# Thresholded attention and leaky-ReLU MoE on one core: fixed issue order, both heads through one clamped fp16 tile, reciprocal sums turned along with the weights

## The chip, the cores and the metric

The kernel runs on one core of one Trainium2 chip. The metric is the device time of one execution in microseconds (us). Each run has a state: slow when it is over 1.5% above the fastest run of the same kernel, else fast.

Engines are named as the profile names them: PE (matmul), PEld (its weight load), DVE (vector), ACT (scalar), POOL (GpSimd), SP (issues most DMAs). A name with a q behind it (SPq) is the engine's queue of DMA issues.

## The reference

Shortened: `scale` is 1 over the root of the head size, and type casts are left out.

```python
def _attn_ref(q, k, v, tau):                     # q, k, v: (8, 8, 576, 64)
    scores = scale * np.matmul(q, k.transpose(0, 1, 3, 2))
    thresh = np.max(scores, axis=-1, keepdims=True) - tau
    scores = np.where(scores >= thresh, scores, -1000000000.0)
    scores = scores - np.max(scores, axis=-1, keepdims=True)
    attn = np.exp(scores)
    attn = attn / (np.sum(attn, axis=-1, keepdims=True) + 1e-09)
    return np.matmul(attn, v)

def _moe_ref(x, w_in, w_out):                    # (4608, 512) x (512, 2048) x (2048, 512)
    h = x @ w_in
    return np.maximum(0.01 * h, h) @ w_out
```

The attention output, heads side by side, is x of the second part.

## The kernel before

The work is cut into 144 steps. A step takes 128 query rows of two heads (or the last 64 rows of four heads): scores on PE, the row maximum on DVE, a thresholded exponential, a DMA transpose of the weights ("turn"), and, LAG = 4 steps later, the weighted sum of v (`pv`) on PE. Units of the MoE part (`h_unit`, `o_unit`) fill PE between the scores. q and k of the next batch are split into a high and a low fp16 part and turned by DMA while a batch runs. A batch has 18 steps; a batch border is where the scores go on to the next batch's q and k.

The two heads of a step go different ways. Head 0 gets an Exp of the fp32 scores on ACT and is masked by a multiply on DVE. Head 1 is scaled into an fp16 tile P, clamped on DVE through its int16 view, and gets its Exp afterwards. POOL then multiplies both by the reciprocal of the row sum.

```python
    def tmax(sc, f):                              # row "maximum", as a minimum of the negated scores
        ...
        nc.vector.tensor_scalar(
            out=halves(ns), in0=sc[:, :, 0:288], scalar1=-C, scalar2=None, op0=AX.mult, op1=AX.min, accum_out=mn)
        nc.vector.tensor_scalar(out=bi, in0=mn, scalar1=tau_f, scalar2=f, op0=AX.add, op1=AX.mult)

    def norm(s):
        ...
        nc.vector.reciprocal(out=rc, in_=sm)
        for h in range(2):
            nc.gpsimd.tensor_scalar(out=W[:, h, :], in0=W[:, h, :], scalar1=rc[:, h : h + 1], ...)
        wt = sb.tile([128, 9, 128], FP16, tag="wt", bufs=LAG, name="wt")
        nc.sync.dma_start(out=wt, in_=W.rearrange("p h k -> p (h k)"), transpose=True)
        ...

    for s in range(NS + LAG + 1):
        ...                                       # credit: how many MoE units this step takes
        if live:
            ...                                   # tiles; those of E and P below are left out too
            scores(s, sc)
            nsa, ba = tmax(sc[0], 1.0)
            nc.scalar.activation(out=E, in_=nsa, func=AF.Exp, bias=ba, scale=-1.0)
            nsb, bb = tmax(sc[1], KD)
            nc.scalar.activation(out=P, in_=nsb, func=AF.Identity, bias=bb, scale=-KD)
        ...                                       # pv(s - LAG), o units, h units
        if 0 <= s - 1 < NS:
            norm(s - 1)
        if live:
            nc.vector.scalar_tensor_tensor(       # mask-multiply of head 0
                out=d["W"][:, 0, :], in0=nsa, scalar=ba, in1=E,
                op0=AX.is_le, op1=AX.mult, accum_out=d["sm"][:, 0:1])
        ...                                       # eviction of pv to xT on ACT; preparation of the next batch
        if live:
            nc.vector.tensor_scalar(out=pi, in0=pi, scalar1=NEG, scalar2=None, op0=AX.max)   # clamp
            nc.scalar.activation(
                out=d["W"][:, 1, :], in_=P, func=AF.Exp, bias=0.0, scale=1.0 / KD, accum_out=d["sm"][:, 1:2])
```

A scheduler orders the instructions of each engine; program order is only its input. At the start all q and k of batch 0 are loaded, split and turned in two halves before the first scores, while POOL issues the loads of v and of both MoE weights.

The names of tiles in the profile: `km`, `qm` are k and q as loaded; `ks`, `qs` their two fp16 parts; `kst`, `qst` these turned, the operands of the scores. `sc` are the scores, `ns` (before) or `sf` (after) the scaled scores, `mn` or `mx` the row minimum or maximum, `bi`, `ba` and `bb` biases made from it, `E` an exponential, `P` the fp16 tile of the clamp. `w` are the weights, `wt` the turned weights, `sm` and `rc` the row sum and its reciprocal, `pv` the weighted sum and `xT` its copy, the input of the MoE part. `win` and `wout` are the MoE weights, `wio` their product, `hp`, `gT`, `op` and `osb` the intermediate and output tiles of the MoE part.

## Time and profile before

| | before |
|---|---|
| time, median of the first 3 runs | 778.84 us (774.13 to 784.93) |
| profiled span | 779.7 us |
| first scores start / last clamp starts | 45.05 / 733.4 us |
| mean granted TensorE clock | 0.914 |

The first part of the page lists the busy time of each engine, its share of the span and its number of instructions. The second part gives forty equal slices; a digit is a share in tenths.

```profile
PE 596.9 (77%) x5520; PEld 345.8 (44%) x5520; DVE 479.0 (61%) x1489; ACT 450.6 (58%) x814; POOL 364.1 (47%) x406
...
PEclk9999988879788598989997899899998999999999
DMA  9999999995895919599478975985479654444511
```

No engine is saturated, and the granted clock dips in the first half. So the time is not the work of one engine. It is what the steps wait for.

Groups of instructions of the kernel before: line, engine, operation, output and inputs with shapes, count, then busy us and mean ns of one, then idle us just before them and who ended it.

```profile
L344 POOL TENSOR_SCALAR w<-w,rc 128x576 f16<-128x576 f16 x288 | 231.6, 816 | 301.6 <-DVE bi L335 175.2
L332 DVE TENSOR_SCALAR_CACHE_REDUCE ns<-sc 128x576 f32<-128x576 f32 x288 | 207.2, 747 | 48.8 <-PE sc L278 44.2
...
L423 DVE SCALAR_TENSOR_TENSOR w<-ns,bi,E 128x576 f16<-128x576 f32 x144 | 162.0, 1125 | 107.9 <-ACT E L411 91.2
...
L432 DVE TENSOR_SCALAR P<-P 128x576 int16<-128x576 int16 x144 | 67.6, 469 | 8.7 <-ACT P L414 8.6
```

DVE spends 162 us on the mask-multiply (L423) and waits another 91 us for E before it. The clamp (L432) has a mean of 469 ns, but its median is 302 and its longest 2460. That is the mark of something that holds it up from outside.

The timeline of the kernel before, an undisturbed step: start, duration, engine, line, operation, and in brackets the idle time before it.

```profile
559.17 1.33 DVE L423 SCALAR_TENSOR_TENSOR w<-ns,bi,E 128x576 f16<-128x576 f32 x1 [0.78 <-ACT E L411]
...
560.43 0.30 DVE L432 TENSOR_SCALAR P<-P 128x576 int16<-128x576 int16 x1
560.65 0.74 DVE L332 TENSOR_SCALAR_CACHE_REDUCE ns<-sc 128x576 f32<-128x576 f32 x1
...
561.33 0.75 DVE L332 TENSOR_SCALAR_CACHE_REDUCE ns<-sc 128x576 f32<-128x576 f32 x1
...
563.05 1.33 DVE L423 SCALAR_TENSOR_TENSOR w<-ns,bi,E 128x576 f16<-128x576 f32 x1 [0.78 <-ACT E L411]
```

The mask-multiply recurs after 3.88 us: two maxima, a wait of 0.78 us for E, the multiply, the clamp, one after the other on DVE. Over the whole run a step takes about 4.8 us, so some 0.9 us per step are lost to other waits.

A count of clamps in a window counts steps. Windows of the kernel before, for the clamp alone: the window and its length, busy us of DVE with the number of clamps (x), then granted clock, DMA share (it can read a little above 1) and GB/s of the core in that window.

```profile
0.00:100.00 100.00, 5.98 (x12) 0.98 1.06 185
100.00:160.00 60.00, 7.47 (x12) 0.81 1.00 164
```

### The profile page before, as it was taken

To read this page: it belongs to the slowest core of one execution; us is meant where nothing else is said; L and a number is where in the kernel's file an instruction comes from. 1 tells how busy PE (TensorE), PEld (TensorE's weight loads), DVE (VectorE), ACT (ScalarE), POOL (GpSimd) and SP (SyncE) were. 2 spreads that over 40 slices of the span, in tenths; PEclk is the share of its full clock that TensorE was granted. 3 is DMA by queue.
4 is the path that set the end of the run, shared out by engine and by line. 5 is a ranking of instruction groups with operands and counts; after the bars stand their busy time and mean duration, and the time that the engine had idled before them with its cause. 6 is when DMAs were issued, how large, how long until landed. Compare 5 with 4: busy or idle time off the path is not lost. (4 is left out here: it accounts for less than half of the span.)

```text
span 779.7 us, 15311 instructions
## 1 busy us (share of the span) xinstructions
PE 596.9 (77%) x5520; PEld 345.8 (44%) x5520; DVE 479.0 (61%) x1489; ACT 450.6 (58%) x814; POOL 364.1 (47%) x406
## 2 busy tenths in 40 slices
PE   0038768688688998778867898679857888888997
PEld 0014334445445454344544455345534545554663
DVE  1058558587384575566656887477755887787501
ACT  2046556675465475575656676576755767676731
POOL 4118557676465443665346633593345333333300
PEclk9999988879788598989997899899998999999999
DMA  9999999995895919599478975985479654444511
GB/s 194 198 189 165 177 183 173 128 182 148 135 172 131 137 30 156 94 180 173 92 119 147 179 117 113 153 144 113 93 120 150 105 103 84 85 90 90 91 41 41
DMA packets 280460, 101.67 MB, mean 130 GB/s; under 512 B 256832, under 2 KB 267072, under 8 KB 280384
## 3 DMA queue, kind: packets, MB, share of 16 engines
q1 hardware_dynamic: 268992, 91.78, 65.8%
q0 software_dynamic: 11392, 8.92, 7.9%
q8 instruction: 43, 0.70, 0.4%
q14 instruction: 33, 0.27, 0.1%
HBM read 36.70 MB, written 9.44 MB: 59 GB/s over the span
## 5 line engine op out<-in xcount | busy, mean ns | idle before, releaser
L344 POOL TENSOR_SCALAR w<-w,rc 128x576 f16<-128x576 f16 x288 | 231.6, 816 | 301.6 <-DVE bi L335 175.2
L278 PE MATMUL sc<-kst,qst 64*128 64x288 f16 x1536 | 175.3, 313 | 103.6 <-DVE ns L332 56.8
L332 DVE TENSOR_SCALAR_CACHE_REDUCE ns<-sc 128x576 f32<-128x576 f32 x288 | 207.2, 747 | 48.8 <-PE sc L278 44.2
L423 DVE SCALAR_TENSOR_TENSOR w<-ns,bi,E 128x576 f16<-128x576 f32 x144 | 162.0, 1125 | 107.9 <-ACT E L411 91.2
L278 PEld LDWEIGHTS <-qst 64*128 64x128 f16 x1536 | 93.5, 101 | 176.0 <-issue 105.5
L170 PE MATMUL hp<-xT,win 128*128 128x256 f16 (+1 forms) x1216 | 157.6, 277 | 11.1 <-ACT gT L188 10.2
L170 PE MATMUL op<-wout,gT 128*128 128x512 f16 x576 | 159.5, 400 | 0.0
L411 ACT ACTIVATE E<-ns,bi 128x576 f16<-128x576 f32 x144 | 110.9, 770 | 69.7 <-DVE bi L335 68.9
L433 ACT ACTIVATE w<-P 128x576 f16<-128x576 f16 x144 | 98.0, 681 | 83.3 <-issue 29.5
L170 PEld LDWEIGHTS <-win 128*128 128x128 f16 x1216 | 115.8, 101 | 56.5 <-issue 21.9
L414 ACT ACTIVATE P<-ns,bi 128x576 f16<-128x576 f32 x144 | 109.6, 761 | 10.3 <-DVE rc L342 7.5
L302 PE MATMUL pv<-wt,v 128*64 128x128 f16 (+1 forms) x1600 | 72.7, 235 | 52.0 <-DMA wt<-w 37.6
L188 ACT ACTIVATE gT<-hp 128x512 f16<-128x512 f32 x144 | 83.2, 581 | 49.8 <-PE hp L170 42.8
L302 PEld LDWEIGHTS <-v 128*64 128x64 f16 x1600 | 54.5, 120 | 88.2 <-issue 69.0
L170 PEld LDWEIGHTS <-gT 128*128 128x128 f16 x576 | 57.8, 101 | 62.2 <-issue 13.1
L432 DVE TENSOR_SCALAR P<-P 128x576 int16<-128x576 int16 x144 | 67.6, 469 | 8.7 <-ACT P L414 8.6
L110 ACT ACTIVATE ks<-km 128x640 f16<-128x640 f32 (+1 forms) x32 | 20.9, 674 | 67.5 <-DMA kst<-ks 55.7
L170 PE MATMUL op<-wio,xT 128*128 128x512 f16 x144 | 58.3, 405 | 2.1 <-DVE osb L207 2.1
L207 DVE COPY osb<-op 128x512 f32<-128x512 f32 x36 | 24.8, 688 | 47.5 <-PE op L170 47.5
L342 DVE RECIPROCAL rc<-sm 128x2 f32<-128x2 f32 x144 | 22.5, 156 | 40.7 <-ACT w L433 39.9
L335 DVE TENSOR_SCALAR bi<-mn 128x1 f32<-128x1 f32 x288 | 39.0, 141 | 0.2
L129 POOL TENSOR_TENSOR ks<-km,ks 128x640 f16<-128x640 f32 (+1 forms) x28 | 38.6, 1395 | 0.7
(31 smaller groups left out, 290.3 us busy)
## 6 DMA issues: line engine op xcount, KB each, us to landing
km<-in_k_dram SPq DMA_DIRECT2D x32, 288.0 KB, 4.7
qm<-in_q_dram SPq DMA_DIRECT2D x32, 288.0 KB, 4.7
out_dram<-osb SPq DMA_DIRECT2D x36, 256.0 KB, 2.7
v<-in_v_dram POOLq DMA_DIRECT2D x16, 160.0 KB, 6.0
wt<-w SPq DMA_TRANSPOSE x144, 3.5
v<-in_v_dram POOLq DMA_DIRECT2D x16, 128.0 KB, 7.3
win<-in_moe_w_in_dram POOLq DMA_DIRECT2D x4, 512.0 KB, 18.5
wout<-in_moe_w_out_dram POOLq DMA_DIRECT2D x4, 512.0 KB, 23.3
```

Of the source, the lines that this page charges most:

```text
L170: nc.tensor.matmul(out=out_, lhsT=lhsT, rhs=rhs, start=start, stop=stop, skip_group_check=True)
L188: nc.scalar.activation(out=G.g[:, ds(u * per, per), :], in_=hp, func=AF.Relu, bias=0.0, scale=0.99)
L278: nc.tensor.matmul(out=sc[h][:, half, 0:288], lhsT=qsts[b, p][r, qi, ds(128 * c, 128)], rhs=ksts[b, p][r, ki, ks_], start=(i == 0), stop=( ...
L302: nc.tensor.matmul(out=pvp[ds(64 * h, 64), p + u, :], lhsT=vt[:, p + u, h, j, :], rhs=wt[:, 4 * h + j, ds(64 * u, n)], start=(j == 0), sto ...
L332: nc.vector.tensor_scalar(out=halves(ns), in0=sc[:, :, 0:288], scalar1=-C, scalar2=None, op0=AX.mult, op1=AX.min, accum_out=mn)
L335: nc.vector.tensor_scalar(out=bi, in0=mn, scalar1=tau_f, scalar2=f, op0=AX.add, op1=AX.mult)
L344: nc.gpsimd.tensor_scalar(out=W[:, h, :], in0=W[:, h, :], scalar1=rc[:, h : h + 1], scalar2=1.0, op0=AX.mult, op1=AX.mult)
L411: nc.scalar.activation(out=E, in_=nsa, func=AF.Exp, bias=ba, scale=-1.0)
L414: nc.scalar.activation(out=P, in_=nsb, func=AF.Identity, bias=bb, scale=-KD)
L423: nc.vector.scalar_tensor_tensor(out=d["W"][:, 0, :], in0=nsa, scalar=ba, in1=E, op0=AX.is_le, op1=AX.mult, accum_out=d["sm"][:, 0:1])
L432: nc.vector.tensor_scalar(out=pi, in0=pi, scalar1=NEG, scalar2=None, op0=AX.max)
L433: nc.scalar.activation(out=d["W"][:, 1, :], in_=P, func=AF.Exp, bias=0.0, scale=1.0 / KD, accum_out=d["sm"][:, 1:2])
```

## The change

Its intent: take POOL out of the weight chain; send both heads the same way, so that one wide clamp serves both and DVE has no mask-multiply; and write the order of each engine's instructions by hand. In its core, with cuts:

```diff
+    ctx.enter_context(tc.manual_schedule())
 ...
+        if 0 < s <= NS:                           # the step before: one clamp and two Exp for both heads
+            anchor[0] = nc.vector.tensor_scalar(out=pi, in0=pi, scalar1=NEG, scalar2=None, op0=AX.max)
 ...
+            for h in range(2):
+                nc.scalar.activation(
+                    out=e["W"][:, ds(576 * h, 576)], in_=e["P"][:, h, :], func=AF.Exp, bias=exp_bias, scale=1.0,
+                    accum_out=sm[:, h : h + 1])
         if live:
-            nsa, ba = tmax(sc[0], 1.0)
-            nc.scalar.activation(out=E, in_=nsa, func=AF.Exp, bias=ba, scale=-1.0)
-            nsb, bb = tmax(sc[1], KD)
-            nc.scalar.activation(out=P, in_=nsb, func=AF.Identity, bias=bb, scale=-KD)
+            sa, ma = smax(s, 0, sc[0])
+            sB, mb = smax(s, 1, sc[1])
 ...
+            nc.vector.tensor_scalar(              # head 0 into P on DVE
+                out=d["P"][:, 0, :], in0=sa, scalar1=ma, scalar2=tau_f, op0=AX.subtract, op1=AX.add)
+            nc.scalar.activation(out=d["P"][:, 1, :], in_=sB, func=AF.Identity, bias=bb, scale=1.0)
 ...
-            nc.gpsimd.tensor_scalar(out=W[:, h, :], in0=W[:, h, :], scalar1=rc[:, h : h + 1], ...)
-        wt = sb.tile([128, 9, 128], FP16, tag="wt", bufs=LAG, name="wt")
+            nc.vector.tensor_scalar(              # reciprocals, spread over a tenth block of W
+                out=e["W"][:, 1152:1280].rearrange("p (h r) -> p h r", h=2),
+                in0=rc.unsqueeze(2).to_broadcast([128, 2, 64]), scalar1=1.0, scalar2=None, op0=AX.mult)
+            turn_w(s - 1)                         # turns 10 blocks
 ...
-                nc.scalar.activation(out=xo, in_=xi, func=AF.Copy, bias=0.0, scale=1.0)
+                nc.vector.tensor_tensor(          # eviction times the turned reciprocals
+                    out=x_, in0=pvp.rearrange("f g (i p) -> f g i p", i=2),
+                    in1=wts[0][:, :, 9, :].rearrange("f g (i p) -> f g i p", i=2), op=AX.mult)
```

Also: output tiles (osb) are copied by ACT instead of DVE; POOL's splitting is tied behind the clamp (`after_anchor`); q and k are loaded and split pair by pair at the start, partly on DVE; the weight loads stand behind POOL's splitting in POOL's queue:

```diff
-    for hb in range(2):
-        load_half(k, kms, "km", 0, hb)
-        load_half(q, qms, "qm", 0, hb)
+    for p in range(NP):
+        load_pair(k, kms, "km", 0, p)
+        load_pair(q, qms, "qm", 0, p)
 ...
             t0 = s0 + 9 * hb                      # when the next batch's loads are issued
 ...
+            t0 = s0 + 1 + 8 * hb                  # when its halves are split and turned
 ...
         at(1 + g // 2, lambda g=g: load_w_in(g))
         at(3 + g // 2, lambda g=g: load_w_out(g))
```

## The prediction

> **What bounds it now.** The busy table (779.7 us span) shows no saturated engine: PE 597, DVE 479, ACT 451, POOL 364 us. There are 144 softmax steps; the first scores start at 45 us, the last end near 729: 4.75 us per step. An undisturbed stretch of the timeline (559 to 567 us) runs at 3.9 us per step, paced by DVE: two 0.68 us maxima, 0.1 of bias, 0.78 waiting for ACT's E, a 1.33 us mask-multiply, the 0.3 us clamp. The other 0.85 us are stalls: in-order queues blocked behind operand preparation and DMA transposes. In the table of waits DVE waits 91 us for E, PE 38 for turned weights and 57 for the maxima, ACT 56 for kst transposes. DMA share is about 1.0 from 50 to 180 us. The granted clock in 2 us windows is 1.00 or 0.50, halved after PE gaps (0.50 at 582 us, after 578 to 582 idle). The Trainium skill, "TensorE: Matmul & The Clock Gate", Part 1, says idleness halves the clock and activity releases it; this trace agrees.
>
> **What changes, per step.**
> - DVE loses the mask-multiply (162 us in all, plus its wait for E) and 25 us of osb copies. It gains P from an fp32 tile (estimate 0.4 us, from the Trainium skill, "VectorE: DVE Perf Modes", the tier table: fp32 SBUF scalar ops run two per cycle), a clamp twice as wide (0.3 to about 0.45), a 128x128 reciprocal broadcast (about 0.25) and, each fourth step, the xT multiply (about 0.75). About 2.9 us busy.
> - ACT trades one fp32 Exp (0.77) for an fp16 Exp with accumulator (0.78), and xT evictions for osb copies: about 3.2 us.
> - POOL loses 232 us of normalisation, so less contention with the clamp (median 302 ns, mean 469, worst 2460).
> - The wt transpose grows from 9 to 10 blocks: about 22 us more DMA in total. All DMA is then about 600 us by the present accounting (74% of 780 plus 22), but late windows move 205 GB/s per unit of share against 176 overall, so about 520 at best: the new second limit.
> - PE work is the same (scores 0.84, pv 0.40, o 1.10, h 0.96 at full clock: 3.3 us per step, about 490 altogether), with fewer gaps, so the clock should rise.
>
> **Critical path.** The weight chain loses POOL (1.46 us plus its queue). DVE's loop falls from 3.9 to about 3.0, and PE (3.3), ACT (3.2) and DMA (3.6) set the pace: 3.9 us per step with residual stalls. Pairwise loads, splitting on DVE, and weight loads queued behind POOL's splitting should bring the first scores from 45 to about 18 us. Tail about 48 as before (same units left after the last scores). Sum: 18 + 144 x 3.9 + 48 = 628 us.
>
> **Predicted: 628 us, 580 to 690.** Faster 0.96, same 0.03, slower 0.01.
>
> **Signs.** Right: first scores before 22 us; POOL busy near 130 us, DVE near 440, ACT near 450; clamp about 0.45 us with few long ones; clock at least 0.95; PE share above 88%; DMA share above 85%. Wrong if pv's waits for wt grow, ACT and DVE lock-step near 4.5 us through clamp and P, or POOL's splitting, now tied to the clamp, makes kst late at batch borders.
>
> **What would make it wrong.** DMA transposes saturating (above 650); fixed order exposing each late semaphore; or a near-dense PE (about 580).

## The result, and the profile after

| | before | after |
|---|---|---|
| time, median (same rounds) | 778.48 us | 667.08 us (664.01 to 670.47) |
| ratio of fast runs, 95% interval | 1 | 0.8564 (0.8491 to 0.8638) |
| mean granted clock | 0.914 | 0.958 |
| first scores / last clamp start | 45.05 / 733.4 us | 16.68 / 618.1 us |

A ratio is the mean time of one kernel's fast runs over that of the kernel before's fast runs of the same rounds, so it is not quite the ratio of the medians.

The page after, its first two parts:

```profile
PE 528.4 (79%) x5584; PEld 317.2 (48%) x5584; DVE 433.9 (65%) x1358; ACT 446.9 (67%) x955; POOL 150.4 (23%) x200
...
PEclk9999979989898989799998989999989998999999
DMA  9999999999999999979996999999998999557301
```

POOL lost 214 us of work and DVE 45, and the clock dips less. The busy share of the DMA is now above 90% in most slices nearly to the end.

Groups after:

```profile
L363 DVE TENSOR_SCALAR_CACHE_REDUCE sf<-sc 128x576 f32<-128x576 f32 x288 | 206.5, 754 | 133.8 <-PE sc L303 122.8
L481 ACT ACTIVATE w<-P 128x576 f16<-128x576 f16 x288 | 193.6, 675 | 29.6 <-DVE P L477 16.9
...
L490 DVE TENSOR_SCALAR P<-sf,mx 128x576 f16<-128x576 f32 x144 | 73.8, 512 | 0.0
...
L477 DVE TENSOR_SCALAR P<-P 128x1152 int16<-128x1152 int16 x144 | 66.0, 459 | 11.0 <-ACT P L492 4.1
...
L496 DVE TENSOR_SCALAR w<-rc 128x128 f16<-128x128 f32 x144 | 32.8, 228 | 5.1
```

The clamp is twice as wide and its mean is no longer than before (459 against 469 ns). The maxima now wait for PE's scores (123 us, before 44), so DVE no longer sets the pace by itself.

The timeline after, a step without a stall:

```profile
400.26 0.91 PE L303 MATMUL sc<-kst,qst 64*128 64x288 f16 x12
...
401.89 0.75 DVE L363 TENSOR_SCALAR_CACHE_REDUCE sf<-sc 128x576 f32<-128x576 f32 x1
...
402.75 0.51 DVE L490 TENSOR_SCALAR P<-sf,mx 128x576 f16<-128x576 f32 x1
...
403.56 0.91 PE L303 MATMUL sc<-kst,qst 64*128 64x288 f16 x12
...
403.68 0.46 DVE L477 TENSOR_SCALAR P<-P 128x1152 int16<-128x1152 int16 x1
...
404.50 0.76 DVE L363 TENSOR_SCALAR_CACHE_REDUCE sf<-sc 128x576 f32<-128x576 f32 x1 [0.36 <-PE sc L303]
```

Scores recur after 3.30 us and PE is dense between them, while DVE waits 0.36 us for them. But the windows, again for the clamp, show that the first steps were slow:

```profile
0.00:100.00 100.00, 4.48 (x9) 0.97 1.09 168
100.00:160.00 60.00, 6.84 (x15) 0.94 0.97 170
```

At 100 us the changed kernel had done 9 steps, the one before 12, although its first scores came 28 us earlier. (Counted by scores instead of clamps, which run a step later in the changed kernel, it is 10 against 13.) From there to the last clamp it did 135 steps in 518 us, 3.84 us each; the kernel before did 132 in 633 us, 4.80 each. The whole gain, and more, is made after 100 us.

The timeline after shows the start:

```profile
16.68 1.62 PE L303 MATMUL sc<-kst,qst 64*128 64x288 f16 x12 [16.68 <-DMA kst<-ks]
...
36.12 19.23 SPq L377 DMA_TRANSPOSE wt<-w  x2
43.32 1.62 PE L303 MATMUL sc<-kst,qst 64*128 64x288 f16 x12 [16.21 <-DMA qst<-qs]
47.87 1.25 ACT L125 ACTIVATE ks<-km 128x640 f16<-128x640 f32 x2 [21.78 <-DMA km<-in_k_dram]
...
66.05 0.75 PE L327 MATMUL pv<-wt,v 128*64 128x128 f16 x10 [8.51 <-DMA wt<-w]
```

PE stands 16 us for a turn of batch 0, ACT 22 us for a load of batch 1 that stands ahead of its Exp in the fixed order, and PE again for turned weights. The issue of two turns took 19 us. A turn of weights lands in 4.4 us at the median, in 20.1 at the worst.

Later there is a stall at every batch border, for instance here:

```profile
489.54 1.44 SPq L144 DMA_TRANSPOSE qst<-qs  x1
...
493.97 1.51 PE L303 MATMUL sc<-kst,qst 64*128 64x288 f16 x12 [2.54 <-DMA qst<-qs]
...
495.51 0.76 DVE L363 TENSOR_SCALAR_CACHE_REDUCE sf<-sc 128x576 f32<-128x576 f32 x1 [4.80 <-PE sc L303]
```

The turn of q that these scores need is issued at 489.54, only 4.4 us before they start. PE idles 2.5 us for it, and DVE then 4.8 us for the scores.

### The profile page after: what moved, and what is told of

Its sections match the earlier page's. It is cut to its first block, busy times and chain, and to the rows that moved or that the text cites. A ratio compares the mean times of both kernels' runs of the same rounds, so it can differ in the third digit from the quotient of the medians.

```text
span 666.1 us, 14773 instructions
## 1 busy us (share of the span) xinstructions
PE 528.4 (79%) x5584; PEld 317.2 (48%) x5584; DVE 433.9 (65%) x1358; ACT 446.9 (67%) x955; POOL 150.4 (23%) x200
## 3 DMA queue, kind: packets, MB, share of 16 engines
q0 software_dynamic: 11392, 8.92, 10.9%
## 4 chain that ended last, share of the span: by engine, by line
PE 51%; DMA 22%; DVE 12%; ACT 9%; SPq 3%; issue 2%; POOL 0%; ACTq 0%
PE op L189 19%; PE hp L189 14%; DMA wt<-w 13%; PE sc L303 10%; DVE sf L363 8%; PE pv L327 5%; DMA qst<-qs 5%; ACT P L492 3%; DMA km<-in_k_dram 3%; ACT w L481 3%; PE wiop L189 2%; DVE P L477 2%; SPq L79 1%; ACT ks L125 1%; PE sc L309 1%
## 5 line engine op out<-in xcount | busy, mean ns | idle before, releaser
L363 DVE TENSOR_SCALAR_CACHE_REDUCE sf<-sc 128x576 f32<-128x576 f32 x288 | 206.5, 754 | 133.8 <-PE sc L303 122.8
L481 ACT ACTIVATE w<-P 128x576 f16<-128x576 f16 x288 | 193.6, 675 | 29.6 <-DVE P L477 16.9
L303 PE MATMUL sc<-kst,qst 64*128 64x288 f16 x1536 | 132.0, 302 | 75.2 <-DMA qst<-qs 45.3
L492 ACT ACTIVATE P<-sf,bb 128x576 f16<-128x576 f32 x144 | 111.4, 773 | 78.0 <-DVE bb L488 72.7
L327 PE MATMUL pv<-wt,v 128*64 128x128 f16 (+1 forms) x1600 | 71.2, 224 | 48.4 <-DMA wt<-w 45.7
L490 DVE TENSOR_SCALAR P<-sf,mx 128x576 f16<-128x576 f32 x144 | 73.8, 512 | 0.0
L477 DVE TENSOR_SCALAR P<-P 128x1152 int16<-128x1152 int16 x144 | 66.0, 459 | 11.0 <-ACT P L492 4.1
L137 POOL TENSOR_TENSOR ks<-km,ks 128x320 f16<-128x320 f32 (+1 forms) x64 | 47.2, 758 | 92.6 <-DVE P L477 61.3
L137 POOL TENSOR_TENSOR qs<-qm,qs 128x576 f16<-128x576 f32 x28 | 35.8, 1278 | 87.0 <-DVE P L477 55.6
L481 ACT ACTIVATION_READ_ACCUMULATOR w<-P 128x1 f32 x288 | 54.8, 190 | 0.0
L496 DVE TENSOR_SCALAR w<-rc 128x128 f16<-128x128 f32 x144 | 32.8, 228 | 5.1
```

Source lines behind the costliest of these rows:

```text
L137: return nc.gpsimd.tensor_tensor(out=dst[:, h], in0=src[:, h], in1=h_[:, h], op=AX.subtract)
L303: nc.tensor.matmul(out=sc[h][:, half, 0:288], lhsT=qsts[b, p][r, qi, ds(128 * c, 128)], rhs=ksts[b, p][r, ki, ks_], start=(i == 0), stop=( ...
L327: nc.tensor.matmul(out=pvp[ds(64 * h, 64), p + u, :], lhsT=vt[:, p + u, h, j, :], rhs=wt[:, 4 * h + j, ds(64 * u, n)], start=(j == 0), sto ...
L363: nc.vector.tensor_scalar(out=halves(sf), in0=sc[:, :, 0:288], scalar1=C, scalar2=None, op0=AX.mult, op1=AX.max, accum_out=mx)
L477: anchor[0] = nc.vector.tensor_scalar(out=pi, in0=pi, scalar1=NEG, scalar2=None, op0=AX.max)
L481: nc.scalar.activation(out=e["W"][:, ds(576 * h, 576)], in_=e["P"][:, h, :], func=AF.Exp, bias=exp_bias, scale=1.0, accum_out=sm[:, h : h ...
```

## The experiments

The questions: why did the start give nothing (39 us over the prediction in all), what holds the steady steps above 3.3 us, and which part of the change made the gain. Every kernel differs from the changed one by the edit shown. Twelve kernels ran, in four groups; kernels of one group share their runs of the kernel before.

| run | edit | median us | ratio to before (95%) |
|---|---|---|---|
| changed kernel | | 667.08 | 0.8564 (0.8491 to 0.8638) |
| x1 | no weight loads (wrong) | 643.65 | 0.8286 (0.8162 to 0.8410) |
| x2 | batch 1 prepared later | 668.62 | 0.8616 (0.8551 to 0.8681) |
| x3 | scheduler's order | 705.09 | 0.9095 (0.9014 to 0.9176) |
| x4 | LAG 6 | 665.05 | 0.8568 (0.8502 to 0.8634) |
| x5 | batches 2 to 7 prepared 3 steps earlier | 646.02 | 0.8238 (0.8190 to 0.8286) |
| x6 | less DMA (wrong) | 647.55 | 0.8288 (0.8259 to 0.8318) |
| x7 | POOL normalises again | 672.66 | 0.8620 (0.8590 to 0.8650) |
| x8 | POOL not tied to the clamp | 674.37 | 0.8631 (0.8607 to 0.8655) |
| x9 | head 0 the old way | 680.24 | 0.8741 (0.8680 to 0.8802) |
| x10 | x5, weights and MoE later | 662.94 | 0.8500 (0.8428 to 0.8571) |
| x11 | x10, batch 1 later | 658.22 | 0.8435 (0.8367 to 0.8503) |
| x12 | x1 and x5 (wrong) | 623.35 | 0.8018 (0.7978 to 0.8058) |

The changed kernel was not run again beside these. A difference to it is one of medians from different groups, and the kernel before's medians range over these groups from 778.1 to 781.9 us: read differences as good to a few us. In the group of x1 to x4 three of the seven runs of the kernel before were slow and left out, and the record calls these four verdicts unclear; the intervals of x1 and x3 still do not touch the changed kernel's, while those of x2 and x4 overlap it.

### x1: no weight loads

```diff
+    nc.gpsimd.memset(w_in16.rearrange("p a b -> p (a b)").bitcast(FP32), 0.0)
+    nc.vector.memset(w_out16.rearrange("p a b -> p (a b)").bitcast(FP32), 0.0)
 ...
-        at(1 + g // 2, lambda g=g: load_w_in(g))
-        at(3 + g // 2, lambda g=g: load_w_out(g))
```

> Wrong on purpose: both MoE weight tiles are set to zero by two memsets at the start and never loaded; all else is as in the changed kernel. Theory A (the 39 us missing at the start go to the weight loads, which fill the DMA while the first steps need it): by 100 us at least 17 steps are done instead of about 10, transposes of the first steps land in about 5 us instead of 15 to 20, time near 635 us. Rival B (the in-order queues block on the next batch's k and q loads and splits, whatever the weights do): time stays above 655 us, ACT still waits about 20 us for km at step 1.

643.65 us, 23 less. The windows of this kernel, for the clamp:

```profile
0.00:100.00 100.00, 7.96 (x16) 1.00 1.01 169
100.00:160.00 60.00, 6.84 (x15) 0.91 1.04 168
```

16 steps are done at 100 us instead of 9, and after that the pace is the same (15 clamps in 60 us in both). So the weight loads cost the start seven steps. The slowest turn of `wt` landed after 10.3 us instead of 20.1; the medians are 4.3 and 4.4. The zeros in the weight tiles did not free the clock: it was 0.964 over the run (0.958 with weights), and 0.91 against 0.94 from 100 to 160 us. It is not all of theory A's claim, which had at least 17 steps and a time near 635 us: ACT still waited 13.0 us for the km of batch 1, so part of what rival B named remains once the weights are gone.

### x2: batch 1 prepared later

```diff
             t0 = s0 + 9 * hb
+            if b == 1:
+                t0 = 10 + 3 * hb
 ...
-            t0 = s0 + 1 + 8 * hb
+            t0 = s0 + (5 if b == 1 and hb == 0 else 1 + 8 * hb)
```

> The k and q loads of batch 1 are issued from step 3 on instead of step 0, and its first half is split from step 5 on instead of step 1; weights as in the changed kernel. Theory B (ACT, and behind it DVE and PE, stand in the fixed order behind the split of a km that has not landed): the 21.8 us wait of ACT for km is gone and time falls by 15 us or more, to 650 or less. Theory A (the DMA is full anyway with weights): the wait moves to the wt transposes and time falls by less than 8 us.

668.62 us: no gain. ACT's wait of 21.8 us is gone (one of 10.5 us for the same km came later, at 70 us), and in its place the issue of three turns took 31.4 us (19.2 for two in the changed kernel), the slowest turn of `wt` landed after 29.9 us, and ACT stood 16.6 us for a bias of DVE, which stood 16.5 us for PE's scores, which stood 17.7 us for a qst. With the weights in the way, reordering what stands behind them moves the wait and does not shorten it. Of the two theories, A is the one that fits this run.

### x3: the scheduler orders again

```diff
-    ctx.enter_context(tc.manual_schedule())
 ...
-        if anchor[0] is not None:
+        if False:
```

> The changed kernel with the scheduler ordering the instructions again (no fixed order, no ties of GpSimd work to the clamp). If the fixed order is a large part of the gain: slower by 5% or more, 700 us or above, with PE clock below 0.94 and steps in the steady part above 4.2 us. If the lighter arithmetic is nearly all of the gain: 655 to 685 us.

705.09 us, 38 more than the changed kernel and some 74 less than the one before. With the scheduler the first clamp came after 50 us, as in the kernel before; DVE waited 93.5 us for ACT's P in front of the clamp (4.1 in the fixed order); and PE's clock was 0.937. From 160 to 580 us it did 99 steps, 4.24 us each, where the changed kernel did 108. At 100 us it had done 12 steps, three more than the changed kernel, so what the fixed order gains is gained after the start. About a third of the 111 us needs the fixed order (with the ties to the clamp, which this run also drops), and two thirds come without it.

### x4: more lag

```diff
-    LAG = 4
+    LAG = 6
-    NWT = 2
+    NWT = 3
```

(with one or two buffers fewer for sf, osb, P, xT and mx, to make room)

> The weighted sum runs 6 steps behind the scores instead of 4 (third buffer of turned weights; sf, osb, P, xT and mx each with one or two buffers fewer to make room). If pv's 46 us of waits for wt are a matter of latency, they fall below 15 us and time by 15 us or more, to 650 or less. If the DMA's throughput sets the pace from 100 to 580 us, time changes by less than 1% and the waits move elsewhere (qst, kst, wt buffers).

665.05 us: within noise. The wait that it was aimed at did shrink: the waits of PE's `pv` for wt fell from 45.7 us to 7.0. The time did not, and the waits of the scores for qst grew from 45.3 to 65.1 us. Taking the wait for turned weights away thus did not make the steps faster. This outcome is the one expected of a DMA whose throughput sets the pace; x5 speaks against that reading. Whether the smaller buffers took back part of what the lag gave was not run apart.

### x5: the next batch prepared three steps earlier

```diff
-            t0 = s0 + 9 * hb
+            t0 = s0 + 9 * hb - (3 if b > 1 else 0)
 ...
-            t0 = s0 + 1 + 8 * hb
+            t0 = s0 + 1 + 8 * hb - (3 if b > 1 else 0)
```

> For batches 2 to 7 the k and q loads, splits and turns all sit three steps earlier; batch 1, at the start, is untouched. If the waits of the scores for qst at the batch borders (4 to 6 us in each of seven places on the chain of waits) are lateness in the fixed order, they vanish for six of them and time falls by 15 to 25 us, to 642 to 652. If the DMA's throughput is the limit from 100 to 580 us, the time moves by less than 1% and the waits go to wt.

646.02 us, 21 less, and correct: this version beats both kernels. (One of its four runs, at 649.38 us, is slow and left out of the ratio.) Who waited for whom: total us, times, longest us. First the changed kernel:

```profile
PE sc L303 <- DMA qst<-qs: 45.3, 10, 16.2
```

then this one:

```profile
PE sc L303 <- DMA qst<-qs: 21.8, 4, 13.9
```

Eight of the ten waits in the changed kernel stand at the borders into batches 1 to 7 (one of 2.2 to 5.4 us at each, and another of 1.1 at one of them). In this run only the border into batch 1, which the edit leaves alone, still has any (4.5 and 0.4 us); the other two are at the start. Windows of the changed kernel, for the clamp, and then of this one:

```profile
160.00:580.00 420.00, 49.26 (x108) 0.95 1.02 173
```

```profile
160.00:580.00 420.00, 52.92 (x116) 0.98 1.05 179
```

Eight more steps fit into the same 420 us, at 3.62 us each instead of 3.89. The clock is higher and the DMA moves more per second. (The profiled run, 639.39 us, is the fastest of the four and 1% below their median, so this window flatters the edit a little.) A DMA share of 1.0 was thus no proof of a full DMA: the same queues carried 3% more when the turns were asked for earlier. The waits at the borders were lateness.

### x6: less DMA

```diff
-        nc.sync.dma_start(out=d["wt"], in_=d["W"], transpose=True)
+        nc.sync.dma_start(out=d["wt"][:, 0:9, :], in_=d["W"][:, 0:1152], transpose=True)
 ...
-                    in1=wts[0][:, :, 9, :] ...
+                    in1=wts[0][:, :, 8, :] ...
 ...
+        if b > 1:
+            vts[b] = vbufs[b % 2]                 # v of batches 2 to 7 is not loaded
```

> Wrong on purpose: the tenth block is computed but not turned (9 blocks again), the eviction multiplies by the ninth, and v of batches 2 to 7 is not loaded. That takes about 4.7 MB of transposes and 3.5 MB of loads off the DMA, some 8% of its bytes, and no instruction off PE, DVE or ACT. If the DMA's throughput sets the pace of the steady part, steps get 5 to 8% shorter there: time 625 to 642. If PE and the interlocks between the engines set it, time stays within 1.5% of the changed kernel.

647.55 us, 20 less: between the two expectations, nearer the first. Bytes on the DMA fell by 8%, time by 3%; from 160 to 580 us a step took 3.72 us instead of 3.89, 4% less, where 5 to 8% were expected of a DMA that sets the pace. A turn of weights also lands a little sooner (4.2 us at the median instead of 4.4), so bandwidth and lateness are not separated by this run alone. The DMA matters in the steady part, but its bytes do not set the pace one for one.

### x7: POOL normalises again

```diff
-            nc.vector.tensor_scalar(out=e["W"][:, 1152:1280]..., in0=rc.unsqueeze(2).to_broadcast([128, 2, 64]), ...)
+            for h in range(2):
+                w_ = e["W"][:, ds(576 * h, 576)]
+                nc.gpsimd.tensor_scalar(out=w_, in0=w_, scalar1=rc[:, h : h + 1], scalar2=1.0, op0=AX.mult, op1=AX.mult)
 ...
-                nc.vector.tensor_tensor(out=x_, in0=pvp..., in1=wts[0][:, :, 9, :]..., op=AX.mult)
+                nc.vector.tensor_copy(out=x_, in_=pvp...)
```

> One part of the change undone: GpSimd normalises the weights again (2 x 144 instructions of about 0.75 us), 9 blocks are turned, the eviction is a plain DVE copy. If taking GpSimd out of the chain[...] is what the tenth block is worth: slower by 2% or more (680 us and above), clamps longer than 0.6 us on average. If the transposes' bytes weigh more: same or faster (650 to 668).

672.66 us, a ratio 0.7% above the changed kernel's with overlapping intervals: not told apart from no difference, and in neither of the two expected ranges. The group lines of this kernel:

```profile
L493 POOL TENSOR_SCALAR w<-w,rc 128x576 f16<-128x576 f16 x288 | 238.7, 841 | 225.3 <-DVE rc L490 224.5
...
L472 DVE TENSOR_SCALAR P<-P 128x1152 int16<-128x1152 int16 x144 | 107.8, 749 | 28.7 <-ACT P L487 26.6
```

The contention is real: the same clamp takes 749 ns on average instead of 459 with POOL's multiplies back, its longest 2924. P from the fp32 tile went from 512 to 598 ns, while the maxima, which read the scores from PE's accumulator memory (PSUM), stayed at 751 (754). The Trainium skill, "SBUF — State Buffer", section "SBUF: two separate sides", says that the port pair shared by GpSimd and Vector is an exclusive lock held for the whole instruction; this agrees. It costs hardly any time here. The likely reasons are that a DVE that waits for PE has room for 0.3 us more per step, and that the tenth block's own bytes are saved; they were not tested apart.

### x8: POOL not tied to the clamp

```diff
-        if anchor[0] is not None:
+        if False:
```

(in `after_anchor` only; the order stays fixed)

> The ties of GpSimd's splitting to the clamp are left out; nothing else. If they keep the wide clamp from waiting behind GpSimd: clamps with a mean above 0.55 us and some above 1.5 us, time slower by 1 to 3%. If they only delay the splits: same or a little faster.

674.37 us, a ratio 0.8% above, again with overlapping intervals. The mechanism was partly wrong: the clamp grew only from 459 to 498 ns, and the longest was 1025, not above 1500. The other DVE instructions in its neighbourhood took more of it (P from 512 to 593 ns, the spread of reciprocals from 228 to 323). A small cost at most; not settled.

### x9: head 0 the old way

```diff
-            nc.vector.tensor_scalar(
-                out=d["P"][:, 0, :], in0=sa, scalar1=ma, scalar2=tau_f, op0=AX.subtract, op1=AX.add)
+            nc.scalar.activation(out=d["E"], in_=sa, func=AF.Exp, bias=ba, scale=-1.0)   # sa: negated scores
 ...
+            nc.vector.scalar_tensor_tensor(       # one step later, so it need not wait for E
+                out=e["W"][:, 0:576], in0=e["ns"], scalar=e["ba"], in1=e["E"],
+                op0=AX.is_le, op1=AX.mult, accum_out=sm[:, 0:1])
```

> One part of the change undone in the fixed order: head 0 goes its old way again (negated scores, Exp on fp32, mask-multiply with accumulator on DVE, one step later so that it need not wait for E), the clamp is 576 wide. DVE gains about 0.5 us per step (mask-multiply 1.13 plus one bias op, less 0.51 for P and 0.15 for the narrower clamp), ACT is unchanged. If DVE's work per step was what the one clamped tile relieved: steps near 4.2 us, time 695 to 720. If the wait of DVE for E, which a fixed order removes anyway, was the larger part: 665 to 685.

680.24 us, 13 more, in the lower of the two ranges. The group line of its mask-multiply:

```profile
L499 DVE SCALAR_TENSOR_TENSOR w<-ns,ba,E 128x576 f16<-128x576 f32 x144 | 116.9, 812 | 0.0
```

It took 812 ns here, not the 1125 of the kernel before, and it waited for nothing. In a fixed order, without POOL's multiplies, the part that the one clamped tile removes is much smaller than the 1.33 us plus 0.78 us that the old timeline showed.

### x10 and x11: weights and MoE later

```diff
-        at(1 + g // 2, lambda g=g: load_w_in(g))
-        at(3 + g // 2, lambda g=g: load_w_out(g))
+        at(4 + g, lambda g=g: load_w_in(g))          # x11: 6 + g
+        at(8 + g, lambda g=g: load_w_out(g))         # x11: 10 + g
 ...
-        credit = min(credit + (1.1 if live else 2.0), 2.5)
-        if s >= 8 and wq:
+        credit = min(credit + (1.2 if live else 2.0), 2.5)
+        if s >= 14 and wq:                            # x11: 16; the turns of w_in and the h and o units start later likewise
```

(both with the edit of x5; x11 also loads batch 1 from step 3 and splits it from step 5)

> A version meant to be better: batches 2 to 7 prepared three steps earlier, the weight loads moved from steps 1 to 4 to steps 4 to 11, the MoE part begins at step 14 instead of 8 and runs at 1.2 units per step. If theory A holds for the start and lateness for the borders, both gains add: 618 to 635. If the weight loads only move their harm to later steps: 640 to 650.

> As x10, with batch 1 loaded from step 3 and split from step 5 as in the run that moved batch 1 later, and the weights at steps 6 to 13, the MoE from step 16. If the first steps still stand behind batch 1's loads in x10: 8 to 15 us faster than x10, 605 to 625. If not: within 1% of x10.

662.94 and 658.22 us: both are slower than x5, which they were meant to improve. At 160 us x10 had done 20 steps and x11 22, x5 25. In x10 the waits of `pv` for wt were 69.3 us (35.1 in x5), the longest 12.2. The slow phase moved to the steps where the loads now stand: in x10 the slowest turn of `wt` landed after 28.6 us. The edit moved the loads and the MoE part together, so their shares are not told apart. Both expectations of x10 were missed, on the slow side. x11 lies within 1% of x10, as expected for the case that the first steps no longer stand behind batch 1's loads there.

### x12: x1 and x5 together

> Wrong on purpose: no weight loads and batches 2 to 7 prepared three steps earlier, the two edits that gained about 23 and 21 us alone. If the loss at the start and the lateness at the batch borders are separate terms, they add: 618 to 628, near the 628 that was predicted without them. If both only relieve the same full DMA, the sum falls short: 634 or more.

623.35 us. The two alone gave 23.4 and 21.1 us; together they give 43.7. Within the noise they add, as separate terms would. Windows of this kernel, for the clamp:

```profile
0.00:100.00 100.00, 7.67 (x16) 0.99 1.02 175
...
160.00:580.00 420.00, 51.78 (x114) 0.98 1.02 174
```

## Why the prediction was right or wrong

The direction and the range held: 667.08 us lies in 580 to 690, and the gain was 111 us where 151 were expected. Its sum was 18 + 144 x 3.9 + 48.

- **Steady pace: right.** 3.9 us per step was expected; 135 steps after 100 us took 3.84. DVE's loop ceased to pace the step, as expected: an undisturbed step is 3.30 us, which is the 3.3 us worked out for PE. The remainder is 0.54 us per step, some 73 us in 135 steps. Late turns at batch borders are shown for 21 us of it (x5); the rest was not traced. The prediction listed late kst at borders among what could go wrong, and in fact qst was the late one. How much the stalls would add to 3.3 us was not derived there, so part of the hit is luck.
- **Tail: right.** 48 us were expected; 48 passed from the last clamp to the end (46 in the kernel before).
- **First scores: right, and the lead was lost by 100 us.** 18 us were expected, 16.7 measured.
- **The term that failed: the start.** The sum lets every step after the first scores run at 3.9 us. From 16.7 to 100 us 21 steps would fit; 9 were done. Twelve steps at 3.9 us are 47 us, less 8 us that the faster later steps give back: the 39 us by which the prediction was short. The step is "Pairwise loads, splitting on DVE, and weight loads queued behind POOL's splitting should bring the first scores from 45 to about 18 us". The prediction counted what this order gives the first scores and left out what it costs the steps behind them. The weight loads did come later (issued from 26 to 57 us, before from 5 to 18), and so they met the first turns of weights. x1 puts 23 us and seven of the twelve steps on them. The other five steps stay lost without the weights; in x1 ACT's 13.0 us for the km of batch 1 and PE's 6.5 us for a qst stand there, but no run took these away. Before, the weight loads ran in the 45 us in which PE waited for its first operands anyway; what they cost there was not measured. That x12 comes out near 628 us does not confirm the sum: it had done 16 steps at 100 us, not 21, and its steps from 160 to 580 us took 3.68 us, not 3.9. The Trainium skill, "DMA: Bandwidth & Descriptors", section "Issuing engines are not separate DMA queues", says that transfers started by different engines interleave on the same 16 DMA engines. The traces agree: beside the loads issued by POOL the slowest turn of `wt` issued by SP took 20.1 us to land, without them (x1) 10.3, at medians of 4.4 and 4.3.
- **DMA as the second limit: half right.** Share above 85% was expected and the page has 83.0 + 10.9%. But x5 gained 21 us without taking a byte away, so the waits at the borders were lateness, and x6 shows that 8% fewer bytes give 3%. The two edits were not run together, so what lateness and bandwidth each cost is not told apart.
- **Costs of single instructions.** Clamp 459 ns (0.45 expected), reciprocal spread 228 (0.25), xT multiply 727 (0.75), DVE 434 us (440), ACT 447 (450): right. POOL was busy for 150 us, not 130. P from the fp32 tile took 0.51 us, not 0.4.
- **Clock: right.** 0.958 against "at least 0.95". **PE share above 88%** is wrong for the span (79%) and right from 100 to 620 us (460 of 520 us); the start makes the difference.

Where the gain came from: the fixed order with its ties, 38 us (x3). The other 74 us come with the scheduler still in place. Undone singly in the fixed order, head 0's way costs 13 us (x9), and the tenth block (x7) and the tie to the clamp (x8) cost less than can be told from noise. These parts do not add up to 74. In the kernel before, the mask-multiply, POOL's multiplies and the waits between them stretch one another (1125 ns before, 812 in x9), so it is likely that undoing one at a time understates them; that was argued, not shown. What the old arithmetic does in a fixed order is open.

## What to carry to other kernels

An earlier first instruction is worth only what the first steps can then run at: ask what the idle start had been hiding, and count finished steps at a fixed time rather than the start of the first one. A wait can look like a full DMA and be a late request; ask for the operand earlier before trying to move fewer bytes. And a cost measured in one order, such as the mask-multiply's 1125 ns and its wait for E, is not what removing it gains in another: in the fixed order it took 812 ns, waited for nothing, and cost 13 us in all.

## What the Trainium skill lacked or had wrong

- "VectorE: DVE Perf Modes", the tier table: it has no fixed term for a short instruction. Its fp32 at two elements per cycle led to an estimate of 0.4 us for 576 elements with a per-partition scalar and fp16 output; measured 512 ns. The section "The TRN2 errata" gives a fixed term of 58 cycles and, beside it, a remark that about 150 were measured; the larger one is nearer here. Estimates from these figures: 576 / 2 + 150 cycles at 0.96 GHz are 456 ns, with 58 cycles 360; for the clamp 1152 / 4 + 150 cycles are 456 ns, measured 459.
- "DMA: Bandwidth & Descriptors", "Issuing engines are not separate DMA queues": says that transfers interleave, but has no figure for casting loads beside transposes. Here the 8.4 MB read for the weights took the slowest landing of a turn of `wt` from 10.3 us (x1) to 20.1, and the run from 644 us to 667.
- "Perfetto Trace Analysis", "Identifying the Most-Contended Engine": calls the occupancy of the DMA misleading because there are 16 engines, but has no figure for the room that a share of 1.0 can leave. Here it was 173 GB/s at a share of 1.02, and 179 at 1.05 once the turns were asked for earlier (x5).
